# Low halves of split queries: from one VectorE operation to a ScalarE pass and a GpSimd subtraction

## The chip, the cores and the metric

The kernel runs on one core of one Trainium2 chip. The metric is device time in microseconds (us), from the start of the execution to its end; lower is better. Engines carry the names of the profile: PE is TensorE's matmul, PEld its weight load, DVE is VectorE, ACT is ScalarE, POOL is GpSimd, SP is SyncE.

## What is computed

Agent attention over 4 batches of 11456 tokens of 128 channels with 49 agents, followed by a mixture of experts with one expert per token:

```python
def _attn_ref(q, k, v, agents):
    def sm(a, b):
        s = scale * (a @ b.transpose(0, 2, 1))
        e = np.exp(s - s.max(-1, keepdims=True))
        return e / (e.sum(-1, keepdims=True) + 1e-09)
    agent_v = sm(agents, k) @ v
    return sm(q, agents) @ agent_v
...
    # per token: gate by softmax of x @ w_gate, its largest expert e
    h = np.maximum(x[mask] @ w1[e], 0.0)
    out[mask] = gate_w[mask, None] * eom[mask, e, None] * (h @ w2[e])
```

## The kernel before, in words

The tokens of a batch are cut into 12 units, 11 of 1024 tokens and one of 192. Three kinds of small product are made unit by unit: scores of keys against the agents (tiles `k_ld`, `ks`), weighted sums of values (`v_ld`, `av`) and scores of queries against the agents (`q_ld`, `qs`). After its scores a query unit goes through a chain of small operations (`q_rest`: maximum, exponential, gating, one-hot, scale factors `smt`), whose transposed result `x_ld` feeds the main products. Main products run over 92 tiles of up to 512 tokens: `mm1` multiplies into the hidden layer (PSUM tiles `h`, four banks), `relu` evacuates each bank in two steps, ACT making the high fp16 part `hh` and DVE the low part `hl`, `mm2` multiplies both parts into `y`, `finish` adds the halves of `y` on ACT and DVE into `os`, and `store` has POOL multiply `os` by `smt` and SP send it out. A ring of 16 `hh` and `hl` tiles (RING, line 1099) stands between `mm1` and `mm2`. Tokens outside a batch's most frequent expert are gathered and done at the end and beside the rest.

**The split.** Scores of keys, and of some queries, are multiplied in fp32. The other 28 query units (those outside WHOLE, line 1083: units 8 to 11 of batch 0 and all of batches 1 and 2; 25 of 1024 tokens and 3 of 192) are split by `split` (line 413) into two fp16 parts that are multiplied in fp16. For one unit ACT makes the sum of squares, one matmul adds it over the channels, DVE turns it into a power of two `s` by two operations on its bits (`scale`, line 477), POOL makes the inverse factors, ACT writes the high part `xh = fp16(s*x)` (line 433), and DVE writes the low part `xl = fp16(s*x - xh)` (line 435) into the first half of the bytes of `x`, the query unit itself (`q_ld` in the trace). At line 436 the parts are handed over; `scores` (line 593) then multiplies, for each of the 8 groups of 128 tokens, `xh` by the agents' high part, `xh` by their low part, and `xl` by the high part. A unit is split no sooner than when the last but one split unit has been scored (line 417).

**The order of the work.** Every engine runs its instructions in the order in which the program is written, and that order comes from a planner that runs while the kernel is built. `Clock` (line 55) keeps a planned time for each engine; the streams of work (generators) offer their next instruction, and `tick` (line 501) takes those whose inputs are planned to be ready and whose engine is not planned to be busy for more than its SLACK (line 61: 400 ns for ACT and DVE, 800 for POOL). LATE (line 60) counts an input from another engine as later than planned: by 600 ns for PE, by 800 ns for POOL, by nothing for ACT and DVE. Costs come from `Engine.cost` (line 164): for n elements DVE is 68 + 1.042 n, plus 65 with three operands; ACT from SBUF is 93 + n/1.2, plus 93 for a scale held in a tile; POOL is 100 + 2.2 n. The splits are one stream (line 1572) of priority 1, behind `relu` and `finish` of the main products (0) and ahead of the query chains (2 and later). All instructions are issued through one helper, so that the trace has line 204 for nearly all of them; tiles tell them apart.

Of the kernel before, what the change touches and what calls it, by code (L numbers as in the profile page):

```python
# [8 lines left out]
F16 = mybir.dt.float16  # L9
# [3 lines left out]
AF = mybir.ActivationFunctionType  # L13
ALU = mybir.AluOpType
# [239 lines left out]
def agent_attention_top1_moe(ctx, tc, qT, kT, v, aT, wg, wo, w1, w2, cst, out):  # L254
    nc = tc.nc
    clk = Clock()
    ACT, DVE, POOL = Engine(clk, "ACT", nc.scalar), Engine(clk, "DVE", nc.vector), Engine(clk, "POOL", nc.gpsimd)
# [28 lines left out]
    def bank(name, dt=F32, w=512, k=None):  # L286

        k = last[0] = first_free()[1] if k is None else k
        t = ps.tile([P, w], dt, tag=f"b{k}", bufs=1, name=name)
        banks[k][1] = t.name  # L290
        return t

    def hold(long=False):

        k = last[0]
        banks[k][0] = False
        if long:
            long_held.append((k, banks[k][1]))
        return k

    def release(k):
        banks[k][0] = True
# [11 lines left out]
    def wait_free(long=False):  # L314
        while True:
            long_held[:] = [x for x in long_held if not banks[x[0]][0] and banks[x[0]][1] == x[1]]

            keep = clk.started and (long or not (Y or resting[0]))
            if n_free() > keep and not (long and len(long_held) > 1) and first_free()[0] <= clk.now() + 50.0:
                return  # L320
            yield None
# [91 lines left out]
    def split(item):  # L413

        kind, b, u = item
        n = UNITS[u][1] * UNITS[u][2]
        while item not in parts or splits[0] - scored_n[0] > 1:
            yield None
        splits[0] += 1
        x = parts.pop(item)  # L420
        xh = wk.tile([P, 1024], F16, name=f"xh{kind}{b}_{u}", tag="xh", bufs=2)
        sq = wk.tile([P, 1], F32, name=f"xq{kind}{b}_{u}", tag="xq")
        yield from ACT.q.activation(xh[:, 0:n], x[:, 0:n], AF.Square, accum_out=sq)
        yield from wait_free()
        r = bank(f"xr{kind}{b}_{u}")
        mark = hold()
        yield from PE.q.matmul(r[:, 0:1], ones16, sq.bitcast(BF16)[:, 1:2], start=True, stop=True)
        s, si = yield from scale(r[:, 0:1], f"xs{kind}{b}_{u}", 14)
        release(mark)
        inv = wk.tile([P, 1], F32, name=f"xi{kind}{b}_{u}", tag="xi", bufs=4)  # L430
        yield from POOL.q.tensor_scalar(inv, si, asi[:, b:b + 1], SCALE if kind == "q" else 1.0, op0=ALU.mult,
                                        op1=ALU.mult)
        yield from ACT.q.activation(xh[:, 0:n], x[:, 0:n], AF.Copy, scale=s)
        xl = x.bitcast(F16)
        yield from DVE.q.scalar_tensor_tensor(xl[:, 0:n], x[:, 0:n], s, xh[:, 0:n], op0=ALU.mult, op1=ALU.subtract)
        halves[item] = xh, xl, inv

    halves = {}
# [2 lines left out]
    def all_splits():  # L441
        for item in ITEMS:
            if item[0] in "kq" and item not in WHOLE:
                yield from split(item)
# [32 lines left out]
    def scale(m, name, e, n=1):  # L477

        k = 190 + e
        b = wk.tile([P, n], I32, name=f"{name}_b", tag=f"pw_b{n}", bufs=4 if n == 1 else 1)  # L480
        yield from DVE.q.tensor_scalar(b, m.bitcast(I32), -0.5, float((k << 23) - (1 << 23)), op0=ALU.mult, op1=ALU.add)
        s = wk.tile([P, n], I32, name=f"{name}_s", tag=f"pw_s{n}", bufs=8 if n == 1 else 1)
        yield from DVE.q.tensor_scalar(s, b, 0x7F000000 + 0x800000, None, op0=ALU.bitwise_and)
        si = wk.tile([P, n], I32, name=f"{name}_si", tag=f"pw_si{n}", bufs=8 if n == 1 else 1)
        yield from POOL.q.tensor_scalar(si, s, -1.0, float(254 << 23), op0=ALU.mult, op1=ALU.add)
        return s.bitcast(F32), si.bitcast(F32)
# [1162 lines left out]
```

## Time and profile before

| what | value |
|---|---|
| median of 3 runs | 1038.69 us (1038.46 to 1045.04) |
| profiled execution, its time | 1040.08 us |
| its span, from first to last instruction | 1038.3 us |
| mean granted TensorE clock | 0.994 |

The profile is one execution. Its first table gives each engine's busy time and share of the span. Groups of instructions are listed by operation and tile ("out<-in", partitions x elements, type, count, busy us, mean ns of one, idle time of the engine before them and what ended it). A table by stretch gives each engine's busy time in a window of the span. The waits name who waited for whom. A PE that is shown as busy may be draining: matmuls overlap, and their ends are modelled.

### The profile page before, as it was taken

To read this page: it belongs to the slowest core of one execution; us is meant where nothing else is said; L and a number is where in the kernel's file an instruction comes from. 1 tells how busy PE (TensorE), PEld (TensorE's weight loads), DVE (VectorE), ACT (ScalarE), POOL (GpSimd) and SP (SyncE) were. 2 spreads that over 40 slices of the span, in tenths; PEclk is the share of its full clock that TensorE was granted. 3 is DMA by queue.
4 is the path that set the end of the run, shared out by engine and by line. 5 is a ranking of instruction groups with operands and counts; after the bars stand their busy time and mean duration, and the time that the engine had idled before them with its cause. 6 is when DMAs were issued, how large, how long until landed. Compare 5 with 4: busy or idle time off the path is not lost. (4 is left out here: it accounts for less than half of the span.)

```text
span 1038.3 us, 28383 instructions
## 1 busy us (share of the span) xinstructions
PE 1007.1 (97%) x10927; PEld 814.5 (78%) x10927; DVE 838.3 (81%) x2203; ACT 643.6 (62%) x1489; POOL 390.3 (38%) x692
## 2 busy tenths in 40 slices
PE   9999999999999999999899999999999999999994
PEld 9998777877688778777688778787777678888794
DVE  2648888889889988988979988889998887768740
ACT  2326667676767776766667767666655565565541
POOL 1302445453224364552233454532333334334321
PEclk9999999999999999999999999999999999999997
DMA  7887645463568534545368454436352335343441
GB/s 259 242 241 226 139 144 130 131 153 108 126 170 184 169 122 110 151 120 163 89 181 170 141 134 139 126 120 174 86 97 73 109 101 151 117 150 93 143 140 50
DMA packets 109114, 147.18 MB, mean 142 GB/s; under 512 B 61420, under 2 KB 71840, under 8 KB 108974
## 3 DMA queue, kind: packets, MB, share of 16 engines
q1 hardware_dynamic: 107630, 143.83, 50.1%
q0 software_dynamic: 1344, 1.49, 0.8%
q8 instruction: 87, 1.43, 0.6%
q14 instruction: 53, 0.43, 0.2%
HBM read 91.86 MB, written 35.17 MB: 122 GB/s over the span
## 5 line engine op out<-in xcount | busy, mean ns | idle before, releaser
L204 PE MATMUL y<-vv,hh 128*128 128x256 f16 (+1 forms) x2880 | 584.4, 273 | 10.0 <-DVE os L204 3.2
L204 PE MATMUL y<-vv,hl 128*128 128x128 f16 (+1 forms) x2880 | 530.9, 219 | 3.3 <-DVE hl L204 2.4
L204 DVE SCALAR_TENSOR_TENSOR hl<-h,hh 128x512 f16<-128x512 f32 (+1 forms) x736 | 448.3, 667 | 70.3 <-ACT hh L204 64.1
L204 ACT ACTIVATE hh<-h 128x512 f16<-128x512 f32 (+1 forms) x736 | 373.8, 592 | 202.7 <-PE h L204 200.9
L204 PEld LDWEIGHTS <-hh 128*128 128x128 f16 (+1 forms) x2880 | 282.4, 98 | 56.9 <-issue 31.8
L204 PEld LDWEIGHTS <-hl 128*128 128x128 f16 (+1 forms) x2880 | 313.5, 109 | 17.0 <-issue 8.6
L204 PE MATMUL h<-x_ld,w 128*128 128x512 f16 (+1 forms) x1472 | 276.8, 376 | 2.0 <-DVE hl L204 1.5
L204 PEld LDWEIGHTS <-w 128*128 128x128 f16 x1472 | 93.0, 99 | 89.7 <-issue 67.6
L204 POOL TENSOR_TENSOR os<-os,smt 128x512 f32<-128x512 f32 (+1 forms) x92 | 96.6, 1050 | 131.6 <-DVE os L204 85.1
L204 PE MATMUL av<-ev,v_ld 128*128 128x50 f32 x720 | 110.1, 251 | 0.4 <-ACT ev L204 0.4
L204 PEld LDWEIGHTS av<-ev,v_ld 128*128 128x128 f32 x720 | 107.1, 191 | 2.1 <-ACT ev L204 0.7
L204 PE MATMUL ks<-at,k_ld 128*128 128x50 f32 x720 | 107.6, 255 | 0.0
L204 ACT COPY ys<-y 128x256 f32<-128x256 f32 x180 | 68.3, 380 | 62.2 <-PE y L204 57.9
L204 PEld LDWEIGHTS ks<-at,k_ld 128*128 128x128 f32 x720 | 104.7, 190 | 1.1 <-ACT S L204 0.2
L204 DVE TENSOR_TENSOR os<-y,ys 128x256 f32<-128x256 f32 x180 | 74.6, 416 | 22.0 <-ACT ys L204 20.9
L204 POOL TENSOR_TENSOR ev<-S,km_o 128x400 f32<-128x400 f32 (+1 forms) x44 | 41.0, 933 | 78.2 <-PE av L204 66.5
L204 POOL TENSOR_TENSOR e<-ef,e 128x392 f16<-128x392 f32 (+1 forms) x48 | 42.5, 885 | 65.7 <-ACT e L204 65.2
L204 PEld LDWEIGHTS qs<-at,q_ld 128*128 128x128 f32 (+1 forms) x308 | 47.6, 191 | 2.4 <-DVE os L204 0.5
L204 PEld LDWEIGHTS <-idle_x 128*128 128x128 f16 x325 | 47.7, 153 | 1.7 <-DVE idle_x L204 1.1
L204 PE MATMUL qs<-at,q_ld 128*128 128x50 f32 (+1 forms) x308 | 48.6, 247 | 0.0
L204 POOL TENSOR_TENSOR sm<-sm,ev 128x400 f32<-128x400 f32 (+1 forms) x33 | 41.0, 1242 | 5.3 <-ACT ev L204 4.3
L204 POOL TENSOR_TENSOR ll<-lL,rr 128x128 f32<-128x128 f32 (+1 forms) x48 | 19.0, 396 | 63.1 <-DVE rr L204 36.8
(258 smaller groups left out, 1367.2 us busy)
## 6 DMA issues: line engine op xcount, KB each, us to landing
q_ld<-qT SPq DMA_DIRECT2D x44, 512.0 KB
v_ld<-v SPq DMA_DIRECT2D x44, 512.0 KB
out<-os SPq DMA_DIRECT2D x88, 256.0 KB
k_ld<-kT SPq DMA_DIRECT2D x43, 512.0 KB
lw_ld<-w SPq DMA_DIRECT2D x28, 512.0 KB
efd<-ef SPq DMA_DIRECT2D x44, 200.0 KB
x_ld<-x_ld SPq DMA_DIRECT2D x176, 38.0 KB
w1t<-w SPq DMA_DIRECT2D x8, 256.0 KB
```

What stands on the lines that cost most here:

```text
L204: return getattr(self.eng, op)(*a, **k)
```

## The change

In `split`, the DVE operation on the low part goes. In its place ACT multiplies the unit by `s` where it lies, in fp32, and POOL subtracts the high part from it and writes fp16 into the first half of the same bytes. Nothing else is edited; the planner reads the new costs and writes a new order of instructions for all engines.

```diff
@@ -430,9 +430,10 @@
         inv = wk.tile([P, 1], F32, name=f"xi{kind}{b}_{u}", tag="xi", bufs=4)
         yield from POOL.q.tensor_scalar(inv, si, asi[:, b:b + 1], SCALE if kind == "q" else 1.0, op0=ALU.mult,
                                         op1=ALU.mult)
+        xl = x.bitcast(F16)
         yield from ACT.q.activation(xh[:, 0:n], x[:, 0:n], AF.Copy, scale=s)
-        xl = x.bitcast(F16)
-        yield from DVE.q.scalar_tensor_tensor(xl[:, 0:n], x[:, 0:n], s, xh[:, 0:n], op0=ALU.mult, op1=ALU.subtract)
+        yield from ACT.q.activation(x[:, 0:n], x[:, 0:n], AF.Copy, scale=s)
+        yield from POOL.q.tensor_tensor(xl[:, 0:n], x[:, 0:n], xh[:, 0:n], op=ALU.subtract)
         halves[item] = xh, xl, inv
```

## Prediction, made before the result was known

> **What bounds the kernel now.** I read the engines' table first, then the stretches, then who ended PE's waits, then the groups by form, and last single stretches of the timeline. The engines:
>
> ```profile
> span 1038.3 us, 28383 instructions
> PE 1007.1 (97%) x10927; PEld 814.5 (78%) x10927; DVE 838.3 (81%) x2203; ACT 643.6 (62%) x1489; POOL 390.3 (38%) x692
> ```
>
> PE is busy for 1007.1 of 1038.3 us, so that 31.2 us is all that any edit to another engine can give back. Where the splits lie is told by the rows of their tile (min/median/max ns, first and last start in us):
>
> ```profile
> L204 PE MATMUL qs<-ah,q_ld x206: 183/184/203, 163.2 to 679.2; 128*128 128x50 f16 x100, 128*96 128x50 f16 x3
> L204 ACT ACTIVATE xhq<-q_ld x28: 384/1078/1107, 108.9 to 643.7; 128x1024 f16<-128x1024 f32 x25, 128x192 f16<-128x192 f32 x3
> L204 DVE SCALAR_TENSOR_TENSOR q_ld<-q_ld,xsq_s,xhq x28: 837/1280/1879, 119.9 to 649.8; 128x1024 f16<-128x1024 f32 x25, 128x192 f16<-128x192 f32 x3
> ```
>
> They run from 108.9 to about 650 us, so I cut the span into four stretches (columns: PE, PEld, DVE, ACT, POOL busy us with counts, then clock, DMA share, GB/s):
>
> ```profile
> 0.00:100.00 100.00, 98.48 (x1027) 93.01 (x1028) 50.55 (x134) 35.73 (x88) 19.35 (x42) 1.00 0.80 239
> 100.00:675.00 575.00, 563.26 (x6448) 446.43 (x6446) 514.80 (x1288) 406.36 (x916) 247.85 (x443) 1.00 0.54 142
> 675.00:925.00 250.00, 246.53 (x2530) 191.78 (x2529) 210.68 (x596) 151.18 (x364) 89.35 (x163) 1.00 0.44 120
> 925.00:1038.00 113.00, 98.84 (x928) 83.31 (x927) 62.23 (x188) 50.32 (x123) 33.77 (x44) 0.95 0.33 103
> ```
>
> In the stretch with splits (second row) PE stands idle for 575.00 - 563.26 = 11.74 us. DVE is at 514.8/575 = 89.5%, ACT at 406.36/575 = 70.7%, POOL at 43.1%. In the third row, without splits, DVE is at 210.68/250 = 84.3% and PE is idle for 3.47 us, which over 575 us would be 8.0. So PE bounds both stretches, DVE is the busiest behind it, and 11.74 us is what the edited stretch holds. Who ended PE's waits there (us in total, times, longest):
>
> ```profile
> PE y L204 <- DVE os L204: 3.2, 3, 1.5
> PE y L204 <- ACT S L204: 2.0, 2, 1.6
> PE y L204 <- DVE hl L204: 1.2, 1, 1.2
> PE y L204 <- ACT avn_sb L204: 0.9, 1, 0.9
> PE y L204 <- DVE s_s L204: 0.9, 2, 0.5
> PE y L204 <- DVE lL L204: 0.7, 1, 0.7
> PE y L204 <- DVE rec L204: 0.7, 1, 0.7
> PE h L204 <- DVE hl L204: 0.7, 3, 0.2
> ```
>
> DVE ended 3.2 + 1.2 + 0.9 + 0.7 + 0.7 + 0.7 = 7.4 us of them and ACT 2.0 + 0.9 = 2.9. No row names the split's own tiles.
>
> **What is removed and added, by size.** The split's rows by form:
>
> ```profile
> L204 DVE SCALAR_TENSOR_TENSOR q_ld<-q_ld,xsq_s,xhq 128x1024 f16<-128x1024 f32 x25 | 34.5, 1379 | 0.4 <-ACT xhq L204 0.4
> L204 ACT ACTIVATE xhq<-q_ld,xsq_s 128x1024 f16<-128x1024 f32 x25 | 29.3, 1173 | 0.0
> L204 DVE SCALAR_TENSOR_TENSOR q_ld<-q_ld,xsq_s,xhq 128x192 f16<-128x192 f32 x3 | 2.7, 908 | 0.0
> L204 ACT ACTIVATE xhq<-q_ld,xsq_s 128x192 f16<-128x192 f32 x3 | 1.4, 475 | 0.0
> ```
>
> DVE loses 34.5 + 2.7 = 37.2 us. The added ACT pass reads the same elements with the same scale and differs only in writing fp32, which no row of this form shows; at the price of its neighbour it adds 29.3 + 1.4 = 30.7 us, 1.17 us a unit. ACT in the stretch goes to 437.1/575 = 76%. For the subtraction on POOL of 1024 elements there is no row either. The nearest:
>
> ```profile
> L204 POOL TENSOR_TENSOR os<-os,smt 128x512 f32<-128x512 f32 x88 | 93.1, 1058 | 124.0 <-DVE os L204 82.2 <-DVE a L204 14.2 <-DVE t L204 6.9
> L204 POOL TENSOR_TENSOR e<-ef,e 128x392 f16<-128x392 f32 x44 | 41.0, 932 | 65.6 <-ACT e L204 65.2
> L204 POOL TENSOR_TENSOR ev<-S,km_o 128x400 f32<-128x400 f32 x40 | 39.5, 988 | 75.7 <-PE av L204 64.0 <-DVE km_o L204 6.1 <-PE xrq L204 3.0
> L204 POOL TENSOR_TENSOR sm<-sm,ev 128x400 f32<-128x400 f32 x30 | 38.1, 1271 | 1.3 <-ACT ev L204 0.3
> ```
>
> Per element they cost 1058/512 = 2.07, 932/392 = 2.38, 2.47 and 3.18 ns, fixed part included. By 1024 that is 2.1 us below and 3.3 us above. I take 2.2: the longest tile, whose fixed part weighs least, is the nearest in size, and the row nearest in kind (`e`, which subtracts an fp16 from an fp32 and writes fp16) carries the fixed part over only 392. So POOL gets about 25 x 2.2 + 3 x 0.5 = 56 us more, 43% to 53% of the stretch. The work that covers POOL is the idle time in front of its own rows (124 us before `os` alone).
>
> **Latency: at nothing.** A unit's chain grows by ACT 1.17 and POOL 2.2 less DVE's 1.38, about 2.0 us, and by up to 0.8 us of the planner's LATE for POOL. How long the low part lies ready before its first use, in the tightest unit of the 28 that I found by pairing all of them in order (unit 4 of batch 2):
>
> ```profile
> 534.45 1.27 DVE L204 SCALAR_TENSOR_TENSOR q_ld<-q_ld,xsq_s,xhq 128x1024 f16<-128x1024 f32 x1
> 545.03 0.18 PE L204 MATMUL qs<-ah,q_ld 128*128 128x50 f16 x1
> ```
>
> It ends at 535.72 and is used at 545.03: 9.3 us. The others lie longer (the last is written from 649.8 and used up to 679.2, by the rows of the tile above), so that 2.8 us more does not reach PE. If that cover were gone, each unit would cost up to 2.8 us, 28 x 2.8 = 78 us; 9.3 us is far from it. The new wait is POOL's for the second ACT pass. Behind it on POOL stand the `os` multiplies (and SP's stores behind those), the `e` subtractions (and SP's transposes), `ev` and `sm`. The planner counts ACT's result as 800 ns late before it writes the POOL instruction, and ACT's 1.17 us row is 0.13 above the planned 93 + 853 + 93 = 1039 ns, so POOL will mostly find its input ready. No DMA is added or moved past another.
>
> **What comes back to DVE.** The trace shows DVE operations with two SBUF inputs standing still for as long as a POOL operation runs, and the reverse:
>
> ```profile
> 305.08 1.04 POOL L204 TENSOR_TENSOR os<-os,smt 128x512 f32<-128x512 f32 x1 [5.62 <-DVE a L204]
> ...
> 305.12 1.02 DVE L204 SCALAR_TENSOR_TENSOR a<-eo,a 128x8 f32<-128x8 f32 x1
> ```
>
> Eight elements took 1.02 us, to 306.14; POOL ended at 306.12. The groups and the medians of the same instructions give the size:
>
> ```profile
> L204 DVE SCALAR_TENSOR_TENSOR a<-eo,a 128x8 f32<-128x8 f32 x44 | 18.3, 415 | 1.9
> L204 DVE TENSOR_TENSOR oh<-lr,rm 128x64 f32<-128x64 f32 x44 | 16.0, 364 | 0.5
> L204 DVE SCALAR_TENSOR_TENSOR lr<-ld,kc 128x64 f32<-128x64 f32 x44 | 15.2, 345 | 3.8 <-issue 2.2 <-POOL ld L204 1.4
> ```
>
> ```profile
> L204 DVE SCALAR_TENSOR_TENSOR a<-eo,a x48: 146/172/1037, 96.0 to 952.0; 128x8 f32<-128x8 f32 x44, 96x2 f32<-96x2 f32 x4
> L204 DVE TENSOR_TENSOR oh<-lr,rm x48: 171/224/1039, 90.7 to 946.6; 128x64 f32<-128x64 f32 x44, 96x16 f32<-96x16 f32 x4
> L204 DVE SCALAR_TENSOR_TENSOR lr<-ld,kc x48: 161/218/1045, 89.8 to 945.9; 128x64 f32<-128x64 f32 x44, 96x16 f32<-96x16 f32 x4
> ```
>
> Held time is busy time less 44 medians: 18.3 - 7.6 = 10.7, 16.0 - 9.9 = 6.1, 15.2 - 9.6 = 5.6, together 22.4 us, caused by some 202 POOL operations of about 1.05 us (the four groups above): 0.11 us each. An operation 2.2/1.05 = 2.1 times as long is met 2.1 times as often and holds 2.1 times as long, 0.49 us each, 12 us in 25; with the operations not counted here (`mx`, `sm`, the other `a`) an estimate of 15. DVE is thus relieved by 37.2 - 15 = 22 us, to 492.6/575 = 85.7%.
>
> What such a hold costs PE now, at a longer one:
>
> ```profile
> L204 DVE TENSOR_TENSOR mx<-S,mx 128x400 f32<-128x400 f32 x36 | 23.0, 639 | 19.9 <-ACT S L204 19.9
> ```
>
> ```profile
> 324.73 1.98 DVE L204 TENSOR_TENSOR mx<-S,mx 128x400 f32<-128x400 f32 x1
> ```
>
> ```profile
> 325.00:330.00 5.00, 5.00 (x58) 4.19 (x54) 5.00 (x9) 4.33 (x9) 1.95 (x4) 1.00 0.68 214
> ```
>
> It took 1.98 us where its group's mean is 0.64, yet PE was busy for all of the 5.00 us around it: the ring of hidden tiles covers a hold of this length there.
>
> The Trainium skill, "SBUF — State Buffer", section "Who interferes with whom", gives the rule of these rows: a VectorE instruction with two SBUF inputs and a GpSimd instruction that reads SBUF block each other for the whole instruction, and whichever is issued first wins. The trace agrees (1.02 us for 8 elements). The removed VectorE operation was such an instruction too, so by that rule the change exchanges a 1.28 us lock for one of 2.2.
>
> **The sum.** DVE going from 89.5% to 85.7% is 0.73 of the way to the 84.3% of the stretch without splits; the same share of the difference in PE's idle time, 0.73 x (11.74 - 8.0), is 2.7 us gained. Its bounds: 0, and the 7.4 us that DVE ended. Against it stands ACT, 30.7 us fuller: at least 30.7/406 of the 2.9 us that ACT ended, 0.2, at most a doubling, 2.9; I take 1.2, between the two, since the pass comes as a piece of 1.17 us ahead of a `hh`. Net -1.5 us: the profiled execution of 1040.08 us, a span of 1038.3 and 1.8 around it, would be 1038.6. It stood 1.39 above the median of the runs; on the median, 1038.69 - 1.5 = **1037.2 us**.
>
> **The rivals.**
> *DVE was the true limit of the stretch.* All 7.4 us that DVE ended go and ACT costs 0.2: 1031.5 us. For it: 89.5% busy, and the longest PE waits end on DVE. Against it: those waits stand mostly at changes of batch (`rec`, `os`, `s_s`), where little of the split lies.
> *Slower: GpSimd's longer lock becomes the wait.* A VectorE operation that meets the subtraction stands still for 1.1 us on average and 2.2 at most, and every `hl` behind it in DVE's queue too, which holds the four `h` banks and so `mm1`. It decides once holds outrun the ring's cover. If half of the time in 25 such holds reached PE, 25 x 1.1 x 0.5 = 13.8 us: 1052.5. For it: 1.02 us holds are common. Against it: the 1.98 us above passed unseen, and DVE gets 37.2 us back. The Trainium skill's "GPSIMD Engine Reference", section "4.1 Engine selection", speaks for this rival: elementwise work on a tile belongs to VectorE, GpSimd being about twice as slow with two inputs. The rows bear the price out, 2.07 ns or more for an element against 1379/1024 = 1.35; they do not show that the slower engine is on the path.
> *Only the order moves.* The planned costs change (DVE -1200, ACT +1039, POOL +100 + 2253 ns a unit), and so does the order of all later instructions. One transition better or worse is the size of the longest waits above, 1.2 to 1.6 us; three of them against the change, 4.5 us: 1043.2.
> *Nothing moves:* every term lies under PE: 1038.7.
>
> **How the numbers follow.** Forecast 0.47 (own range 1033 to 1041); DVE the limit 0.12; GpSimd's lock 0.14; the order alone 0.15; nothing 0.12. A measurement of this kernel tells about 1% from no change: 1028.3 and 1049.1. Faster by more needs more than all waits that DVE ended; a third of that rival with a lucky order, 0.05. Slower by more is two thirds of the lock and a little of the order, 0.12. The rest, 0.83, is within 1%. The range is 1030 to 1050: it holds the DVE rival's time and all but the worst of the lock, leaving out some 0.15.
>
> **What would show it.** POOL gains a group `q_ld<-q_ld,xhq`, 25 of 2.1 to 2.4 us; ACT a third pass of about 1.17; DVE's busy time falls by about 22 us to 816, not by 37; the means of `a`, `oh`, `lr` and `mx` rise; PE's idle time between 100 and 675 us is 9 to 11 us; no PE wait names `q_ld`. A PE wait for `q_ld` would prove the latency wrong; POOL above 3 us a unit its price; `h` or `y` waiting for `hl` by 5 us or more would be the lock.

## The result and the profile after

The changed kernel takes 1048.97 us (median of 10 runs, 1046.63 to 1057.76), the kernel before in the same series 1039.88 (median of 10): a ratio of 1.0087, 95% interval 1.0064 to 1.0109. It is slower by 9 us, and its shortest run (1046.63) is longer than the longest of the kernel before (1045.26). The time lies in the stated range, and within 1%, but the forecast was 1.5 us faster.

The profiled execution took 1046.85 us, a span of 1045.1. The page of the changed kernel, engines, and its stretches (PE, PEld, DVE, ACT, POOL busy us with counts):

```profile
span 1045.1 us, 28395 instructions
PE 1009.4 (97%) x10927; PEld 813.9 (78%) x10927; DVE 821.0 (79%) x2175; ACT 669.3 (64%) x1517; POOL 426.3 (41%) x720
```

```profile
0.00:100.00 100.00, 98.47 (x1027) 92.99 (x1027) 50.59 (x134) 35.78 (x88) 19.42 (x42) 1.00 0.79 239
100.00:675.00 575.00, 559.09 (x6364) 440.98 (x6363) 488.92 (x1242) 426.71 (x931) 277.37 (x462) 1.00 0.54 141
675.00:925.00 250.00, 245.60 (x2534) 191.55 (x2533) 213.83 (x602) 151.67 (x365) 92.71 (x167) 1.00 0.43 116
```

VectorE is relieved (838.3 to 821.0 us) and yet PE stands idle for 575.00 - 559.09 = 15.91 us of the stretch with splits, where it was 11.74. The first 100 us are the same. The new rows, by form:

```profile
L204 POOL TENSOR_TENSOR q_ld<-q_ld,xhq 128x1024 f16<-128x1024 f32 x25 | 53.5, 2138 | 29.9 <-ACT q_ld L204 29.0 <-PE h L204 0.7
L204 ACT ACTIVATE q_ld<-q_ld,xsq_s 128x1024 f32<-128x1024 f32 x25 | 28.9, 1157 | 0.7
```

The prices are those of the prediction (2.2 and 1.17). Most of the time is lost in one stretch. It is shown here from 225 to 350 us, first before, then after:

```profile
225.00:350.00 125.00, 122.17 (x1405) 97.37 (x1404) 114.24 (x303) 91.92 (x209) 43.00 (x89) 1.00 0.59 151
```

```profile
225.00:350.00 125.00, 118.61 (x1337) 93.45 (x1335) 105.87 (x277) 91.22 (x201) 48.02 (x86) 1.00 0.56 146
```

Here batch 0 ends, batch 1 begins and the keys of batch 2 are scored. PE gets through 1337 matmuls where it did 1405, and stands idle for 6.39 us where it was 2.83. Counted along the main products, the first `y` of tile 16 comes 1.1 us later than before (at 252 us), that of tile 24 5.7 (at 332), that of tile 64 7.6 (at 730). Who ended PE's waits between 100 and 675 us, after:

```profile
PE h L204 <- DVE hl L204: 3.6, 15, 0.4
PE y L204 <- DVE os L204: 3.1, 4, 1.4
PE y L204 <- DVE w L204: 2.0, 2, 1.6
PE y L204 <- DVE lL L204: 1.8, 3, 0.7
PE xrq L204 <- ACT xhq L204: 1.4, 1, 1.4
```

No row names `q_ld`: no wait of PE for the low part shows. PE waits for VectorE in many small places, although VectorE has less to do. That put the planner's new order under suspicion, beside the operations.

### The profile page after: what moved, and what is told of

The parts are those of the page before. It is cut to its first block, busy times and chain, and to the rows that moved or that the text cites. A ratio compares the mean times of both kernels' runs of the same rounds, so it can differ in the third digit from the quotient of the medians.

```text
span 1045.1 us, 28395 instructions
## 1 busy us (share of the span) xinstructions
PE 1009.4 (97%) x10927; PEld 813.9 (78%) x10927; DVE 821.0 (79%) x2175; ACT 669.3 (64%) x1517; POOL 426.3 (41%) x720
## 5 line engine op out<-in xcount | busy, mean ns | idle before, releaser
L204 POOL TENSOR_TENSOR q_ld<-q_ld,xhq 128x1024 f16<-128x1024 f32 (+1 forms) x28 | 55.1, 1968 | 29.9 <-ACT q_ld L204 29.0
L204 ACT COPY S<-ks 128x400 f32<-128x400 f32 (+1 forms) x48 | 23.0, 480 | 32.4 <-PE ks L204 32.4
```

The lines of the kernel that those rows point to most:

```text
L204: return getattr(self.eng, op)(*a, **k)
```

## The experiments

**Theories.** A: the loss is the new order of instructions, not the operations. B: the operations cost it, by ScalarE's longer queue or by GpSimd's lock on VectorE. All ratios are to the kernel before, run beside each kernel on the same chip; its median was between 1036.2 and 1039.5 us from series to series.

| run | order of | operations of | median us | ratio, 95% interval |
|---|---|---|---|---|
| e1 | before | after | 1070.14 | 1.0277, 1.0249 to 1.0305 |
| e2 | after | before | 1047.84 | 1.0075, 1.0054 to 1.0096 |
| e3 | plan of the split's DVE operation +200 ns | before | 1039.42 | 0.9983, 0.9966 to 1.0000 |
| e4 | plan of the same -200 ns | before | 1042.83 | 1.0031, 1.0013 to 1.0049 |
| e5 | own | ScalarE pass, DVE subtracts | 1045.64 | 1.0080, 1.0051 to 1.0109 |
| e6 | own | GpSimd subtracts, no pass; scaling of the low part left out | 1038.79 | 1.0017, 0.9994 to 1.0040 |
| e7 | own | no low part; the high part in its place | 1674.58 | 1.6138, 1.6081 to 1.6195 |
| e8 | plan with measured prices | after | 1041.98 | 1.0044, 1.0023 to 1.0066 |
| e9 | ScalarE pass reserved | before | 1043.65 | 1.0073, 1.0056 to 1.0090 |
| e10 | the same, 800 ns | before | 1044.93 | 1.0090, 1.0069 to 1.0112 |
| e11 | before | before and a ScalarE pass | 1052.42 | 1.0150, 1.0137 to 1.0163 |
| e12 | ScalarE pass reserved | before and a ScalarE pass | 1045.71 | 1.0110, 1.0086 to 1.0134 |
| e13 | GpSimd reserved | before | 1046.18 | 1.0093, 1.0059 to 1.0127 |
| e14 | own | after, pass in two halves | 1034.81 | 0.9972, 0.9950 to 0.9994 |
| e15 | own | after, in 16 steady units | 1032.12 | 0.9956, 0.9939 to 0.9972 |
| e16 | own | after, in the other 12 units | 1044.86 | 1.0071, 1.0043 to 1.0099 |
| e17 | own | e15 with halves | 1035.84 | 0.9988, 0.9967 to 1.0009 |
| e18 | e15's, measured prices | as e15 | 1032.36 | 0.9962, 0.9941 to 0.9984 |

**The granted clock beside the ratios.** The mean granted TensorE clock differs from execution to execution, and the time goes with it: of the kernel before, beside e13 to e16, 14 executions at 0.996 took 1035.11 to 1036.68 us and five at 0.991 took 1040.17 to 1042.11. The kernels met different clocks, e16 for instance 0.988 to 0.994 and never 0.996, so part of a ratio can be the clock. The executions at 0.994, of each kernel and of the kernel before in the same series:

| run | its executions at 0.994, us | kernel before at 0.994, us |
|---|---|---|
| e2 | 1045.23, 1046.25, 1047.97 | 1038.57 to 1042.27 (8) |
| e9 | 1041.61, 1043.05 | 1037.66, 1039.13 |
| e10 | 1044.04 | 1037.66, 1039.13 |
| e13 | 1042.61, 1042.80 | 1037.79 |
| e15 | 1031.25 to 1034.59 (7) | 1037.79 |
| e16 | 1039.06 | 1037.79 |
| e18 | 1031.15 to 1036.32 (7) | 1038.11, 1038.92 |

At one clock e2 still loses 6 to 7 us, e9, e10 and e13 some 4 to 6, and e15 and e18 still gain. Of e16's 7.4 us, 1.3 are left at 0.994 and about 3 at 0.991 (1044.14 beside the 1040.17 to 1042.11). These are few executions, and whether an order can lower the clock itself is not shown.

**Order against operations (e1, e2).** e1 reserves the old VectorE operation in the plan and puts the two new operations where it stood:

```diff
+        ins, outs = [x[:, 0:n], s, xh[:, 0:n]], [xl[:, 0:n]]
+        yield "DVE", ins, outs, 0
+        clk.issue("DVE", ins, outs, DVE.cost("scalar_tensor_tensor", ins, outs, {}), 150.0)
+        nc.scalar.activation(x[:, 0:n], x[:, 0:n], AF.Copy, scale=s)
+        nc.gpsimd.tensor_tensor(xl[:, 0:n], x[:, 0:n], xh[:, 0:n], op=ALU.subtract)
-        yield from DVE.q.scalar_tensor_tensor(xl[:, 0:n], x[:, 0:n], s, xh[:, 0:n], op0=ALU.mult, op1=ALU.subtract)
```

> The changed kernel's operations (ScalarE pass and GpSimd subtraction) in the order of the kernel before: the planner is told of the old VectorE operation at the old price, and the two new operations are put where it stood. Theory A, the loss of 9 us is the new order that the planner wrote: ratio to the kernel before 0.996 to 1.002 (1036 to 1041 us). Theory B, the operations themselves cost it (ScalarE's longer queue, GpSimd's lock on VectorE): 1.006 to 1.011 (1045 to 1051 us).

e2 reserves ScalarE and GpSimd as in the changed kernel, and runs the old operation where the subtraction stood:

```diff
+        ins, outs = [x[:, 0:n], s], [x[:, 0:n]]
+        yield "ACT", ins, outs, 0
+        clk.issue("ACT", ins, outs, ACT.cost("activation", ins, outs, {}), 120.0)
+        ins, outs = [x[:, 0:n], xh[:, 0:n]], [xl[:, 0:n]]
+        yield "POOL", ins, outs, 0
+        clk.issue("POOL", ins, outs, POOL.cost("tensor_tensor", ins, outs, {}), 120.0)
+        nc.vector.scalar_tensor_tensor(xl[:, 0:n], x[:, 0:n], s, xh[:, 0:n], op0=ALU.mult, op1=ALU.subtract)
```

> The old VectorE operation in the order of the changed kernel: the planner is told of the ScalarE pass and the GpSimd subtraction at their prices, VectorE does the work where the subtraction stood. Theory A (order): 1.006 to 1.012 of the kernel before, since the order is the changed one; VectorE's operation comes unplanned on top. Theory B (operations): 0.998 to 1.003.

In the traces e1 has the order of the kernel before and e2 that of the changed kernel: on PE, ACT, DVE and POOL every instruction but the split's own stands in the same place. e2 comes out at 1.0075 with the old operations: 0.0075 x 1039.45 = 7.8 us are lost with the new order, and the interval of the changed kernel (1.0064 to 1.0109) overlaps its own (1.0054 to 1.0096). They are lost in the same stretch:

```profile
225.00:350.00 125.00, 120.29 (x1348) 94.90 (x1346) 106.66 (x288) 86.20 (x199) 36.96 (x83) 0.99 0.59 148
```

Its operation, by form:

```profile
L441 DVE SCALAR_TENSOR_TENSOR q_ld<-q_ld,xsq_s,xhq 128x1024 f16<-128x1024 f32 x25 | 33.0, 1322 | 0.0
```

The plan of e2 has no room for this operation, so the 7.8 us are the price of the new order with 33.0 + 2.3 = 35 us of unplanned VectorE work in it (2.3 for the three short units); e2 doesn't tell how much is the order's own. With that, theory A holds for the result: putting the old operations back doesn't bring the time back. It fell in its other half: e1, the new operations in the old order, is not the kernel before but 2.8% slower, outside what either theory expected. In e1 GpSimd stands still for the ScalarE pass that the plan doesn't know:

```profile
POOL os L204 <- DVE os L204: 68.9, 31, 3.8
POOL ev L204 <- PE av L204: 65.3, 31, 4.7
POOL e L204 <- ACT e L204: 60.7, 16, 26.9
POOL q_ld L439 <- ACT q_ld L438: 59.8, 24, 4.5
```

That is 2.5 us each time, with everything behind it on GpSimd's queue, and 1.17 us a unit that ScalarE's plan lacks. So the operations are far from free where the plan has no room for them.

**Is any new order a loss (e3, e4)?** The kernel before with +200.0 and -200.0 ns in the planned cost of the split's VectorE operation, nothing else.

> The kernel before, instruction for instruction, but the planner is told that the split's VectorE operation takes 200 ns more than before (28 times), so that the order of the rest moves. Theory A in its general form (any new order is a draw of several us): more than 3 us away from the kernel before, either side. Theory B: within 2 us, 1037 to 1041.

> As the one with 200 ns more, but 200 ns less. Theory A in its general form: more than 3 us away from the kernel before on either side, and not the mirror image of the other. Theory B: within 2 us of the kernel before.

-1.8 and +3.2 us. Orders do differ without any instruction being changed, by less than the 7.8.

**Halves of the change (e5, e6, e7).**

```diff
 # e5
+        yield from ACT.q.activation(x[:, 0:n], x[:, 0:n], AF.Copy, scale=s)
+        yield from DVE.q.tensor_tensor(xl[:, 0:n], x[:, 0:n], xh[:, 0:n], op=ALU.subtract)
 # e6
+        yield from POOL.q.tensor_tensor(xl[:, 0:n], x[:, 0:n], xh[:, 0:n], op=ALU.subtract)
 # e7
+        xl = xh
 # all three
-        yield from DVE.q.scalar_tensor_tensor(xl[:, 0:n], x[:, 0:n], s, xh[:, 0:n], op0=ALU.mult, op1=ALU.subtract)
```

> Half of the change: the ScalarE pass over the unit is added, and VectorE subtracts the high part as before in one operation (now without the scale), both known to the planner. Where the new order loses 8 us: if the added ScalarE work in the plan does it, 1.005 to 1.012 of the kernel before; if GpSimd's does it, 0.998 to 1.004; if it is a draw, anything within 0.996 to 1.010 and no sum with the other half.

> The other half: GpSimd subtracts the high part from the unit as it was loaded, so the scaling of the low part is left out; there is no second ScalarE pass. If GpSimd's 2.1 us operations in the plan are what loses, 1.005 to 1.012 of the kernel before; if ScalarE's pass is, 0.996 to 1.002, since VectorE is relieved.

> The relief of VectorE alone: the low part is not made at all, and the high part stands in its place in the third product (that part of the computation is left out; the matmuls are all there). The prediction's term for the relief of 22 us, 2.7 us gained, would become 2.7 x 37/22 = 4.5 us: 0.995 to 0.997. If VectorE's operation lies wholly under TensorE: 0.998 to 1.002. If every new order loses: above 1.003.

The ScalarE half shows the whole loss (1.0080), the GpSimd half none (1.0017); each has an order of its own. e7's time missed every expectation, and says nothing of the question: the loop behind the main work runs on for the better part of 1674.58 - 1037.74 = 637 us, presumably because with its gates more tokens fall outside the experts that the program provides for. Its first part can still be read:

```profile
100.00:675.00 575.00, 565.37 (x6481) 449.89 (x6479) 485.79 (x1265) 406.78 (x920) 232.79 (x444) 1.00 0.53 143
```

With VectorE's operation gone and nothing in its place PE is idle for 9.63 us instead of 11.74: 2.1 us less, for 29 us less on VectorE. But e7 has an order of its own too, and e3 and e4, with every operation in place, stand at 575.00 - 562.88 = 12.12 and 575.00 - 561.83 = 13.17 us. What the relief is worth by itself is not separated from that.

**The changed kernel in another order (e8).** The measured prices in the plan (ScalarE +130 ns, GpSimd -220 ns a unit), every instruction the same.

> The changed kernel, instruction for instruction, with the planner told the measured prices of the two new operations (ScalarE +130 ns, GpSimd -220 ns a unit). If the loss is a draw of the order: more than 3 us away from the changed kernel, either way. If it lies in the two operations' places in any order: within 2 us of it, 1.007 to 1.011 of the kernel before.

1.0044 against 1.0087, intervals that only just meet (1.0023 to 1.0066, 1.0064 to 1.0109): about half the loss went with the order alone. e5 had made ScalarE's pass the suspect; this made it doubtful again.

**ScalarE's pass, planned and run, each by itself (e9 to e12).** The pass is the high part made twice, so that nothing new waits for it. e9 and e10 reserve it (1039 and 800 ns) and do not run it; e11 runs it and does not reserve it; e12 does both.

```diff
 # e9; e10 with - 240.0; e12 with the last line, ahead of the high part
+        ins, outs = [x[:, 0:n], s], [xh[:, 0:n]]
+        yield "ACT", ins, outs, 0
+        clk.issue("ACT", ins, outs, ACT.cost("activation", ins, outs, {}), 120.0)
+        nc.scalar.activation(xh[:, 0:n], x[:, 0:n], AF.Copy, scale=s)
```

> The kernel before, operation for operation, but the planner reserves ScalarE for one more pass of 1039 ns per split, ahead of the high part, and nothing is run there. If reserving ScalarE makes an order that loses by itself: 1.004 to 1.010 of the kernel before. If each order is a draw: anywhere from 0.997 to 1.009. If only running the pass costs: 0.998 to 1.002.

> As the one before, with 800 ns reserved in place of 1039: a second draw. If reserving ScalarE loses systematically: about three quarters of the other one's loss, within 2 us. If it is a draw: no relation, more than 3 us apart.

> The high part is made twice by ScalarE, one pass behind the other, and the planner knows of one only: the order of all engines is that of the kernel before, with 28 more passes of 1.17 us on ScalarE. If ScalarE's added work is hidden, 0.998 to 1.002 of the kernel before; if unplanned work on ScalarE reaches TensorE, at most 28 x 1.17 = 31 us: 1.005 to 1.03.

> The high part made twice by ScalarE, both passes planned; VectorE as before. If the pass costs through the order alone, the time of the kernel that plans it and does not run it, within 2 us. If running it costs too, more than that kernel by 3 us or more.

Reserving costs 1.0073 and 1.0090, no less for the smaller reservation (the intervals overlap); running it on top costs 1.0110 - 1.0073 = 0.0037, 3.8 us of the 28 x 1.17 = 33 us, with intervals that touch (1.0086 to 1.0134, 1.0056 to 1.0090). e9 and e12 have the same order in their traces. Not planned, the pass costs 16 us. The plan is worth having, and the order that it makes costs no less than the work.

**Is it ScalarE, the piece, or the place (e13 to e16)?**

```diff
 # e13, ahead of the old operation; nothing is run
+        ins, outs = [x[:, 0:n], xh[:, 0:n]], [sq]
+        yield "POOL", ins, outs, 0
+        clk.issue("POOL", ins, outs, 100.0 + 2.2 * n, 120.0)
 # e14, in the changed kernel
-        yield from ACT.q.activation(x[:, 0:n], x[:, 0:n], AF.Copy, scale=s)
+        for o in (0, n // 2):
+            yield from ACT.q.activation(x[:, o:o + n // 2], x[:, o:o + n // 2], AF.Copy, scale=s)
 # e15 (e16: if not)
+        if (b == 1 and u < 8 or b == 2 and 2 < u < 7):
+            yield from DVE.q.scalar_tensor_tensor(xl[:, 0:n], x[:, 0:n], s, xh[:, 0:n], op0=ALU.mult, op1=ALU.subtract)
+        else:
+            yield from ACT.q.activation(x[:, 0:n], x[:, 0:n], AF.Copy, scale=s)
+            yield from POOL.q.tensor_tensor(xl[:, 0:n], x[:, 0:n], xh[:, 0:n], op=ALU.subtract)
```

> The kernel before, operation for operation, but the planner reserves GpSimd for 2353 ns per split ahead of VectorE's operation, and nothing is run there. If any reservation loses as much as ScalarE's: 1.005 to 1.010 of the kernel before. If it is ScalarE's in particular: 0.997 to 1.004, as the other edits of the plan gave.

> The changed kernel with the ScalarE pass cut into two of 512 elements, so that the planner may put an evacuation of the hidden layer between them. If the length of the piece is the price: 1.000 to 1.005 of the kernel before. If ScalarE's time in the plan is, or the order is a draw: 1.005 to 1.011, the fixed part of one more instruction on top.

> The change in 16 of the 28 split units only: the 12 that are split where keys are scored too (units 0 to 7 of batch 1, 3 to 6 of batch 2) keep VectorE's operation. If the loss belongs to the changes of batch, where ScalarE is fullest: 0.997 to 1.003 of the kernel before. If it belongs to ScalarE's time anywhere: 16/28 of 1.009, 1.004 to 1.007.

> The change in the other 12 units only. If the loss belongs to the changes of batch: 1.006 to 1.011 of the kernel before. If it belongs to ScalarE's time anywhere: 12/28 of 1.009, 1.002 to 1.006.

e13 refutes the suspicion against ScalarE: GpSimd reserved and not used loses as much, 1.0093. It loses in the same stretch as the changed kernel, and here the wait has a name, the banks of `y` that come free late:

```profile
225.00:350.00 125.00, 116.07 (x1309) 91.91 (x1308) 106.19 (x282) 85.70 (x197) 38.66 (x81) 0.99 0.58 143
```

```profile
PE y L204 <- DVE os L204: 8.6, 6, 4.0
```

(The second is e13's PE waits in that stretch.) Not every order loses there. e9 is not behind in this stretch, and loses before and after it (1365 matmuls between 100 and 225 us where the kernel before has 1393, 3636 between 350 and 675 where it has 3657):

```profile
225.00:350.00 125.00, 123.30 (x1411) 98.44 (x1410) 111.74 (x301) 90.93 (x206) 41.19 (x91) 1.00 0.58 152
```

e14 and e15 then show that the operations need not lose at all. In halves the pass costs ScalarE more, and the kernel is faster than before:

```profile
L204 ACT ACTIVATE q_ld<-q_ld,xsq_s 128x512 f32<-128x512 f32 x50 | 36.4, 731 | 0.6
```

The 12 units that keep VectorE's operation in e15 get their high parts from 210 to 346 and from 500 to 563 us in the trace of before, about where keys are scored (287 to 350 and 518 to 574). With the change in the 16 others, the steady units, 1.0 - 0.9956 is 4.6 us gained; in those 12 alone, 1.0071 is 7.4 us lost by the medians, of which 1 to 3 us are left at one clock (the table of clocks). So most of e16's loss can't be put down to these units. The stretch with splits of e15:

```profile
100.00:675.00 575.00, 568.39 (x6510) 450.68 (x6510) 501.56 (x1283) 421.22 (x937) 267.60 (x461) 1.00 0.56 143
```

```profile
PE y L204 <- DVE avs L204: 1.2, 2, 0.9
PE y L204 <- DVE lL L204: 1.1, 2, 0.7
PE y L204 <- DVE s_s L204: 1.1, 1, 1.1
```

PE is idle for 6.61 us, down from 11.74, and no wait for `hl` or for `os` at a `y` is left among the longest.

**Is e15 a lucky order (e17, e18)?** e17 is e15 with the halves of e14; e18 is e15 with the measured prices of e8.

> The change in the 16 steady units only, with the ScalarE pass in two halves there. If both effects are of the operations (VectorE relieved, shorter pieces on ScalarE): 0.992 to 0.996 of the kernel before. If they are draws of the order: anything from 0.994 to 1.008.

> The change in the 16 steady units only, the same instructions, with the planner told the measured prices (ScalarE +130 ns, GpSimd -220 ns): another order. If relieving VectorE in the steady units gains by itself: 0.994 to 0.998 of the kernel before, as the first order gave 0.9956. If that was a lucky order: 0.998 to 1.008.

e18 repeats the gain in another order: 0.9962 beside 0.9956. e17 gives 0.9988, no difference that this measurement tells. The best kernels of the study are e15 and e18, 1032.1 and 1032.4 us against 1036.6 and 1036.9 for the kernel before beside them.

**What is settled and what is open.** Shown: the two operations need not lose, since e8 with the same instructions in another order loses half as much and e14, with the pass in two pieces, gains; the changed kernel's order loses with the old operations put back (7.8 us, their VectorE work unplanned); plans with an empty reservation lose with the old operations (e9, e10 and e13, some 4 to 6 us at one clock). In the changed kernel, in e2 and in e13 most of the loss arises between 225 and 350 us, in e9 it does not. The change in the 16 steady units gains in two orders. Not settled: which placement in the losing orders sets PE back. The traces name a different late tile each time (`hl` and `w` in the changed kernel, `os` in e13). That the units at the changes of batch lose is not shown: e16 is one order, most of its loss goes at one clock, and e14 has the change in all units and is faster than before. How much of e15's gain is the operations' and how much its order's was not separated.

## Why the prediction was wrong

**What bounds the kernel** was right: PE at 97% before and after, and 31 us of idle time as the limit of any gain.

**Prices** were right. GpSimd 2.138 us for 2.2, ScalarE 1.157 for 1.17.

**Latency at nothing** was right. The tightest unit is now unit 5 of batch 1:

```profile
329.49 2.13 POOL L204 TENSOR_TENSOR q_ld<-q_ld,xhq 128x1024 f16<-128x1024 f32 x1 [4.12 <-ACT q_ld L204]
...
339.02 0.18 PE L204 MATMUL qs<-ah,q_ld 128*128 128x50 f16 x1
```

339.02 - 331.62 = 7.4 us are left. "POOL will mostly find its input ready" was wrong: the row of the new operation above shows 29.0 us of waiting for the ScalarE pass, in 17 cases. It did not decide: e2 loses without it.

**What comes back to DVE** was near. The means of the held operations rose; after:

```profile
L204 DVE TENSOR_TENSOR mx<-S,mx 128x400 f32<-128x400 f32 x36 | 25.0, 694 | 21.9 <-ACT S L204 21.8
L204 DVE SCALAR_TENSOR_TENSOR lr<-ld,kc 128x64 f32<-128x64 f32 x44 | 18.6, 422 | 4.4 <-issue 2.2 <-POOL ld L204 2.2
L204 DVE SCALAR_TENSOR_TENSOR a<-eo,a 128x8 f32<-128x8 f32 x44 | 18.5, 422 | 2.6 <-ACT eo L204 0.3
L204 DVE TENSOR_TENSOR oh<-lr,rm 128x64 f32<-128x64 f32 x44 | 16.7, 380 | 0.8
```

Against the rows of before these are +2.0, +3.4, +0.2 and +0.7 us. The largest rise stands at `rr`, which the estimate did not count: 17.8 us for 44 where it was 13.2. All in all VectorE is 838.3 - 821.0 = 17.3 us emptier, where the prediction had 22. GpSimd got 426.3 - 390.3 = 36.0 us fuller and not 56: its own operations are held less without VectorE's, which the prediction left out. The additions `sm` went from a mean of 1271 ns to 1031, and to 1035 in e7, where nothing takes the place of VectorE's operation.

**The sum failed**, in what it left out. It took the order for given and moved busy times in it. The term that decided stood among the rivals as "Only the order moves", with no place in the sum, at 4.5 us and a chance of 0.15; e2 lost 7.8 us with that order and the old operations, VectorE's unplanned. Its size was taken from the longest single waits, three of 1.5 us. In the changed kernel part of the loss came otherwise, by many short waits (15 for `hl`, 0.4 at most), and PE was 68 matmuls behind after 125 us; in e13 it came as six waits of up to 4.0 us. The terms that the sum did have fared unevenly. The relief, 2.7 us forecast, was not seen by itself (2.1 us less idle in e7, for 29 us of VectorE and in another order). ScalarE's term, 1.2 us with 2.9 at most, was short by the one comparison of a pass run and not run in the same order, e12 against e9: 3.8 us, with intervals that touch. The rival "GpSimd's longer lock" is not what happened: e2 loses as much with VectorE's own 1.32 us operation back in place of GpSimd's 2.14, and e6, with GpSimd's operations (and without the scaling), does not lose. That the time lies within the range is luck: the room above was left for that lock.

## What to carry to other kernels

Where a planner writes the order, a change of two operations is a change of every instruction behind them, and the order can be worth more than the operations: here planned costs alone moved the time by -0.2 to +0.9%, and the change where it did good gained 0.4%, in two orders. Set the granted clocks of the executions beside a difference this small, as e16 shows. Cross the two before judging an operation: the old operations in the new order, and the new in the old. Moving work to a fuller engine pays where it is known to have room, so try it by stages of the kernel, and test a gain in a second order before believing it.

## What the runs showed of the hardware

GpSimd's two-input subtraction of fp16 from fp32 took 548 ns for 192 elements and 2131 for 1024 (shortest and median of the row below), 1.90 ns for each further element. An operation with one tensor input from SBUF is held as well: `rr`, a multiplication of 8 elements by a scalar that lies in a tile, took up to 1.745 us in the changed kernel beside a median of 0.224.

```profile
L204 POOL TENSOR_TENSOR q_ld<-q_ld,xhq x28: 548/2131/2283, 121.1 to 658.0; 128x1024 f16<-128x1024 f32 x25, 128x192 f16<-128x192 f32 x3
```

```profile
L204 DVE TENSOR_SCALAR rr<-d,s_s x48: 132/224/1745, 83.1 to 946.3; 128x8 f32<-128x8 f32 x44, 96x2 f32<-96x2 f32 x4
```

```profile
409.04 2.12 POOL L204 TENSOR_TENSOR q_ld<-q_ld,xhq 128x1024 f16<-128x1024 f32 x1
...
409.44 1.75 DVE L204 TENSOR_SCALAR rr<-d,s_s 128x8 f32<-128x8 f32 x1
```

The longest `rr` ran to 411.19 us, the subtraction that stood in its way to 411.16. That it has one tensor input is read from its code (`d256` times `s3`). The Trainium skill, "SBUF — State Buffer", section "Who interferes with whom", names such operations in a 2-port mode beside those with two SBUF inputs; this row agrees, though no view here shows the mode.
